# A planner's constant for one transfer's part of the DMA queue: 0.9 in place of 1.1

## The chip, the cores and the metric

The kernel runs on one core of one Trainium2 chip. The metric is the device time of one execution in microseconds, the median of several; three executions of the kernel before took 909.14, 910.29 and 910.53 us. Five engines work beside each other: TensorE (PE in the profile) multiplies matrices into PSUM, VectorE (DVE) and ScalarE (ACT) do elementwise work, and SyncE (SP) and GpSimd (POOL) issue the DMA transfers. Each engine works through its own instructions in the order in which the program was written down, and waits on semaphores for what others have to finish first.

## The reference

Two stages, with 8 sequences of 3,072 tokens, width 256, query and key width 64 and hidden width 1,024:

```python
scores = (1 / S) * z @ z.T                # per sequence, 3072 x 3072
attn   = maximum(scores, 0) ** 2
x      = u * (attn @ v)                   # gated attention, 3072 x 256
h1, h2 = x @ w1, x @ w2                   # 24576 x 1024 each
out    = maximum(h1, h2) @ w_out          # 24576 x 256, float32
```

## The kernel before

A *step* is one block of 512 query tokens of one sequence; there are 48 steps, six to a sequence, numbered through from 0. The scores of a step are made in pairs of 128-token key blocks (`score`, PE), go through a relu and a square (`relu` and `square`, ACT or DVE) and land in SBUF tiles of four key blocks, `a_sb` (a *group*). Since `z @ z.T` is symmetric, a group above the diagonal isn't computed again for the step below it: SyncE transposes it there with a DMA (`turn`, tile `aT`), one transfer for each pair of key blocks. Below, "turn 2:12" is the transfer that turns step 2's key blocks 12 and 13; it goes into group 2 as step 3 reads it, and 2:12 and 2:14 together make up that group. The block on the diagonal has a smaller transfer of its own ("turn 3:diag"). So steps 3, 4 and 5 read what steps 0 to 2 (and the steps just before them) have turned, and nothing is turned for steps 0 to 2.

The products with `v` of steps 0 to 2 are plain matmuls (`plain`). From step 3 on they are made with seven products of quarters in place of eight, in four passes over the groups, `Xa`, `Xb`, `Ya`, `Yb`; the first two read the tiles themselves, the last two also sums of quarters that DVE makes (`es`, jobs `S2` to `S4`), and folded `v` (`lf`). For step 3 the groups are read in the order 0, 1, 4, 5, 2, 3 (the diagonal last), for step 4 in the order 0, 1, 2, 5, 3, 4, for step 5 in the order 5, 0, 1, 2, 3, 4.

The result of a step is multiplied by `u`, which SyncE has turned as well (`uT`), on DVE into `xT` (function `scaled`, `mul_uT`, L295), which also makes the two PSUM accumulators free for the next step's products. A few steps later come the first layer (`d`), a relu (`g`), the second layer (`o`), the copy into `o_sb` (`oc` on ACT, of which there are two buffers, L75) and the store to DRAM, again by SyncE (`store`). `max(h1, h2)` is made as `relu(x (w1 - w2)) @ w_out + x (w2 @ w_out)`; the product `w2 @ w_out` (`w2o`, 16 matmuls in step 3) needs `w2` turned by SyncE (`w2T`, twice the size of a turn).

SyncE's DMAs all go through one queue, in the order in which SyncE issues them (`sp_dma`, L103). The loads of `u`, `v`, `z` and the weights are issued by GpSimd (`load`, L107), most of them tied to a matmul that has to be done first.

No order is written by hand but PE's. Everything else is a *job* with the engines that may do it, a duration, its dependencies and the buffers that it uses. `find_orders` (L1758) is a list scheduler that is run while the program is built: it always takes the job that can begin first, prefers earlier due times among those that can begin within 400 ns, and keeps a clock for each engine and one for the DMA queue (`dma_free`). `settle` (L1773) reckons when a transfer is done: the queue's clock moves on by `DMA_PART` times the transfer's time alone, and SyncE is held back while that clock is over 4,500 ns ahead. `share_wide` (L1835) gives the 19 wide buffers (tiles `a_sb` and `aT`) to their uses by the begins and ends so reckoned; 24 rounds are reckoned, and the order of the best is used (L1879).

```python
dma_free[0] = max(dma_free[0], begin + DMA_START[...]) + DMA_PART * j.dma
j.done = dma_free[0] + DMA_END
if "SP" in j.ways:
    idle_from["SP"] = max(begin + SP_ISSUE, dma_free[0] - DMA_AHEAD)
```

Of the kernel before, what the change touches and what calls it, by code (L numbers as in the profile page):

```python
# [11 lines left out]
def kernel(  # L12
# [185 lines left out]
    TURN, TURN_LAG, UT_LAG = 1750, 4000, 7000  # L198

    DMA = dict(turn=1180, uT=1130, zT=4220, w2T=3800, store=1940, v=1680, u=1680, z=3130, w1=4100, w2=3000, wo=3500)  # L200
    DMA_SMALL, DMA_PART = 970, 1.1
    DMA_START, DMA_END, DMA_AHEAD, SP_ISSUE = {"SP": 870, "POOL": 1770}, 1330, 4500, 1450
    FIRST_LOADS = {("v", 0, 0): 0, ("v", 0, 1): 1200, ("v", 0, 2): 2500, ("v", 0, 3): 3700, ("v", 0, 4): 4900, ("v", 0, 5): 7700, ("u", 0): 6300}

# [1777 lines left out]
```

## Time and profile before

| What | Value |
|---|---|
| Three executions | 909.14, 910.29, 910.53 us |
| Median | 910.29 us |
| Profiled execution, its own time | 914.21 us |
| Profiled execution, span from first to last instruction | 912.4 us |
| PE busy | 892.1 us (98%) |
| DVE busy | 790.0 us (87%) |
| ACT busy | 756.2 us (83%) |
| Mean granted TensorE clock | 0.996 |
| DMAs issued by SyncE | 394, of them 279 turns of score tiles, 48 `uT`, 51 stores |

The span is the time from the first to the last instruction of the profiled execution; its own time of 914.21 us has 1.8 us around that. A row of the timeline gives start, duration, engine, line, operation, what is written and read, how many instructions are merged into the row, and in square brackets the idle time before it and what ended it. SyncE's rows are the issues of transfers; what the profile calls "DMA to landing" is the time from the begin of an issue until the data has landed.

### The profile page before, as it was taken

Reading aid. Unit: us, or ns where it says so; the run is one execution under the profiler, and the core shown is the slowest. Engines: PE = TensorE matmul, PEld = TensorE weight load, DVE = VectorE, ACT = ScalarE, POOL = GpSimd, SP = SyncE. Lnnn points to the kernel's source line nnn. Section 1 sums busy time; section 2 is a strip of 40 time slices with the busy share of each in tenths; the row PEclk is TensorE's granted clock in tenths of the full one; section 3 lists DMA queues with packets and bytes.
Section 4 is the critical chain, followed back from the end, with each engine's and each line's share of the span. In section 5 each row is a group of like instructions: output and inputs, shape, how many; then the busy total and the mean of one; then the engine's idle time right before and its main releaser. Section 6 shows DMA issues by size and latency. Waiting matters only on the chain.

```text
span 912.4 us, 37105 instructions
## 1 busy us (share of the span) xinstructions
PE 892.1 (98%) x16333; PEld 745.5 (82%) x16333; DVE 790.0 (87%) x1703; ACT 756.2 (83%) x944; POOL 58.4 (6%) x115
## 2 busy tenths in 40 slices
PE   9999799999999999999999999999999999999998
PEld 3368688887888888888788888888888898888885
DVE  6777678988989999999899899998999899989970
ACT  7967699778997899888997889977999779997634
POOL 2101000010000000001000010000000001000000
PEclk9999899999999999999999999999999999999999
DMA  9999999999999999999999999999989999999711
GB/s 156 130 167 175 186 182 173 175 163 159 153 169 190 164 183 149 164 185 167 165 146 164 183 169 151 166 169 173 183 138 178 179 178 152 170 160 162 123 61 70
DMA packets 382930, 146.65 MB, mean 161 GB/s; under 512 B 361264, under 2 KB 362928, under 8 KB 382768
## 3 DMA queue, kind: packets, MB, share of 16 engines
q1 hardware_dynamic: 366208, 114.54, 79.3%
q0 software_dynamic: 16560, 29.74, 23.5%
q8 instruction: 127, 2.08, 1.0%
q14 instruction: 35, 0.29, 0.1%
HBM read 59.77 MB, written 25.17 MB: 93 GB/s over the span
## 4 chain that ended last, share of the span: by engine, by line
PE 74%; DVE 12%; DMA 6%; ACT 4%; issue 2%; SPq 0%; POOL 0%; DVEq 0%; POOLq 0%; ACTq 0%
PE s_ps L87 37%; PE acc L87 37%; DMA v_sb<-in_v_dram 3%; DMA aT<-a_sb 3%; DVE es L290 2%; ACT a_sb L276 2%; DVE es L293 2%; DVE a_sb L293 1%; ACT g_sb L276 1%; DVE xT L297 1%; DVE e L290 1%; DVE e L293 1%; DVE a_sb L284 1%; DVE o_sb L293 1%; DVE gs L293 1%
## 5 line engine op out<-in xcount | busy, mean ns | idle before, releaser
L87 PEld LDWEIGHTS <-v_sb 64*128 64x128 bf16 (+1 forms) x4464 | 336.1, 94 | 68.9 <-issue 15.2
L276 ACT ACTIVATE a_sb<-s_ps 128x1024 bf16<-128x1024 f32 x337 | 303.8, 943 | 45.4 <-PE s_ps L87 43.8
L87 PEld LDWEIGHTS <-lf 64*128 64x128 bf16 x3240 | 266.2, 94 | 21.9 <-issue 7.3
L87 PE MATMUL acc<-es,v_sb 64*128 64x256 bf16 x2160 | 279.0, 269 | 0.0
L87 PE MATMUL acc<-es,lf 64*128 64x256 bf16 x1080 | 246.6, 269 | 0.3
L87 PE MATMUL acc<-a_sb,lf 64*128 64x256 bf16 x1224 | 233.1, 269 | 1.0 <-issue 1.0
L87 PE MATMUL s_ps<-xT,w_sb 64*128 64x512 bf16 (+1 forms) x1484 | 214.0, 377 | 0.0
L282 ACT ACTIVATE a_sb<-a_sb 128x1024 bf16<-128x1024 bf16 (+1 forms) x217 | 211.1, 993 | 2.3
L276 ACT ACTIVATE g_sb<-s_ps 128x1024 bf16<-128x1024 f32 x187 | 185.9, 1024 | 8.6 <-PE s_ps L87 6.9
L87 PE MATMUL acc<-aT,lf 64*128 64x256 bf16 x936 | 180.1, 271 | 3.8 <-DMA aT<-a_sb 3.1
L87 PE MATMUL acc<-a_sb,v_sb 64*128 64x256 bf16 (+1 forms) x1352 | 145.4, 280 | 3.2 <-DVE e L290 2.3
L87 PE MATMUL s_ps<-zT 64*128 64x512 bf16 (+2 forms) x774 | 122.5, 337 | 6.1 <-DVE o_sb L290 2.9
L290 DVE TENSOR_TENSOR es<-aT 128x1536 bf16<-128x1536 bf16 (+1 forms) x117 | 106.5, 933 | 1.3 <-DMA aT<-a_sb 1.2
L87 PEld LDWEIGHTS <-gs 64*128 64x128 bf16 x2688 | 99.1, 94 | 9.5 <-issue 1.3
L87 PEld LDWEIGHTS <-w_sb 64*128 64x128 bf16 (+1 forms) x1488 | 80.9, 94 | 26.0 <-POOLq L95 1.0
L87 PEld LDWEIGHTS <-g_sb 64*128 64x128 bf16 x2336 | 91.6, 94 | 10.4 <-POOLq L95 7.1
L284 DVE TENSOR_TENSOR a_sb<-a_sb 128x1024 bf16<-128x1024 bf16 (+1 forms) x121 | 74.8, 625 | 25.9 <-ACT a_sb L276 25.9
L87 PE MATMUL acc<-aT,v_sb 64*128 64x256 bf16 x936 | 89.5, 272 | 0.0
L293 DVE TENSOR_TENSOR es<-a_sb 128x512 bf16<-128x512 bf16 x198 | 79.1, 421 | 9.6 <-PE acc L87 9.5
L87 PE MATMUL s_ps<-wf_sb,gs 64*128 64x128 bf16 x2016 | 81.2, 216 | 0.5 <-issue 0.5
L87 PE MATMUL s_ps<-w_out_sb,g_sb 64*128 64x128 bf16 (+1 forms) x1664 | 78.8, 226 | 0.0
L290 DVE TENSOR_TENSOR es<-a_sb 128x1024 bf16<-128x1024 bf16 x108 | 72.4, 687 | 0.0
(84 smaller groups left out, 1079.6 us busy)
## 6 DMA issues: line engine op xcount, KB each, us to landing
out_dram<-o_sb SPq DMA_DIRECT2D x47, 512.0 KB, 5.5
v_sb<-in_v_dram POOLq DMA_DIRECT2D x48, 256.0 KB, 6.0
u_sb<-in_u_dram POOLq DMA_DIRECT2D x48, 256.0 KB, 5.7
aT<-a_sb SPq DMA_TRANSPOSE x230, 5.3
z_sb<-in_z_dram POOLq DMA_DIRECT2D x7, 384.0 KB, 7.0
w_sb<-in_moe_w_dram POOLq DMA_DIRECT2D x2, 512.0 KB, 10.3
uT<-u_sb SPq DMA_TRANSPOSE x48, 5.6
a_sb<-a_sb SPq DMA_TRANSPOSE x45, 5.5
```

Of the source, the lines that this page charges most:

```text
L87: newest[0] = pin(nc.tensor.matmul(*args, **kw)).ins
L276: pin(nc.scalar.activation(out_ap, in_ap, AF.Relu))
L282: pin(nc.scalar.activation(ap, ap, AF.Square))
L284: pin(nc.vector.tensor_mul(ap, ap, ap))
L290: pin(nc.vector.tensor_add(*args))
L293: pin(nc.vector.tensor_sub(*args))
L297: nc.vector.scalar_tensor_tensor(out=out_ap, in0=in0, scalar=c2, in1=in1, op0=ALU.mult, op1=ALU.mult)
```

## The change

One constant of the planner. With it the planner believes that a transfer takes 0.9 of its time alone in the queue, where it believed 1.1 before: 1,062 ns for a turn in place of 1,298 ns. No instruction is added, removed or made larger.

```diff
-    DMA_SMALL, DMA_PART = 970, 1.1
+    DMA_SMALL, DMA_PART = 970, 0.9
```

The order of PE and of GpSimd stays as it was. The order of SyncE changes in two ways. In the opening, that is up to step 6, it is another order. These are the transfers from the sixth on, before and after, with their places in SyncE's order:

```
place   before     after          place   before     after
  6     1:14       1:14             22    3:16       zT (two)
  7     1:16       1:16             23    3:18       3:16
  8     w2T        1:18             24    0:22       3:18
  9     uT 2       1:20             25    uT 4       0:22
 10     1:18       w2T              26    1:20       2:20
 11     2:12       uT 2             27    1:22       4:diag
 12     2:14       1:22             28    5:diag     2:22
 13     3:diag     0:20             29    2:20       3:20
 14     uT 3       2:12             30    2:22       uT 4
 15     0:16       2:14             31    store 0    5:diag
 16     0:18       0:16             32    3:20       3:22
 17     2:16       3:diag           33    4:20       store 0
 18     2:18       uT 3             34    3:22       4:20
 19     zT (two)   0:18             35    4:22       store 1
 20     0:20       2:16             36    uT 5       4:22
 21     4:diag     2:18             37    6:diag     6:diag
```

From step 7 on the only changes are that of two neighbours in SyncE's order one goes ahead of the other, some five times in each sequence: a `uT` ahead of a turn or of a store, or a turn ahead of a store and a `uT`.

On DVE and ACT the order changes in the opening alone: eight squares of steps 3 to 7 change between the two engines, the first two sums for group 2 of step 3 (`S2`, `S3`) stand ahead of sums for groups 4 and 5, and three folds of `v` of the second sequence stand 28 places earlier. From the middle of step 6 on, both orders are the same as before. The wide buffers are given to 259 of their uses otherwise than before.

## The prediction

> **What bounds the kernel now.** I read the page's busy shares and slices first, then the chain of waits of PE, then the windows around each wait, and last SyncE's rows in the opening.
>
> ```profile
> span 912.4 us, 37105 instructions
> PE 892.1 (98%) x16333; PEld 745.5 (82%) x16333; DVE 790.0 (87%) x1703; ACT 756.2 (83%) x944; POOL 58.4 (6%) x115
> PE   9999799999999999999999999999999999999998
> ```
>
> PE is busy for 892.1 of 912.4 us, and of the 40 slices only the fifth, 91 to 114 us, falls below 9 tenths. So no order of the other engines can save much in the body, but it can lose there, and in the opening (before 114 us) it can do both. These are PE's rows at the waits, and the clock behind them:
>
> ```profile
> 83.09 0.28 PE L87 MATMUL acc<-aT,lf 64*128 64x256 bf16 x2 [0.48 <-DMA aT<-a_sb]
> 103.30 0.39 PE L87 MATMUL s_ps<-zT 64*128 64x512 bf16 x2 [2.18 <-ACT o_sb L287]
> 106.88 0.40 PE L87 MATMUL acc<-aT,lf 64*128 64x256 bf16 x2 [2.65 <-DMA aT<-a_sb]
> 106.00:112.83 6.83, 5.95 (x49) 0.50 1.10 227
> 102.66 1.07 ACT L287 COPY o_sb<-s_ps 128x512 f32<-128x512 f32 x2 [4.39 <-DMA out_dram<-o_sb]
> ```
>
> PE waits 0.48 us for a turn in step 4, 2.18 us for a PSUM pair, and 2.65 us for turn 3:22. The second wait is a transfer's too: ACT's copy, which gives the pair free, waited for store 0 out of `o_sb`. After the two the granted clock is 0.50 from 106.00 to 112.83 us (PE busy 5.95 us there), which costs half of 5.95, 2.97 us. So the opening loses 0.48 + 2.18 + 2.65 + 2.97 = **8.28 us** to late transfers. That is what the change can win, against what it newly makes late.
>
> **The body.** From step 7 on PE, DVE, ACT and GpSimd keep their orders, and SyncE only swaps neighbours. The swapped transfer with the least time to spare, by my reading of all of them, is uT 11:
>
> ```profile
> 213.62 4.24 SPq L104 DMA_TRANSPOSE uT<-u_sb  x1
> DMA to landing us min/median/max: 10.4/10.4/10.4
> 236.93 0.68 DVE L297 SCALAR_TENSOR_TENSOR xT<-e,uT 128x512 bf16<-128x512 f32 x1
> ```
>
> It lands at 224.0 and is read at 236.93, 12.9 us later; a swap moves a transfer by one place, which the issues below put at 1.3 us. If SyncE waits at a `uT` that it reaches too early, the neighbour behind it waits as well, by no more than those 12.9 us allow. At the begins that the trace shows, the new sharing of the wide buffers makes no job after 110 us wait longer. I cost the body at nothing; the cover is this slack, and without it each late transfer would cost PE what it is late by.
>
> **The opening, before.** SyncE issues almost without a pause from 29 to 122 us and is blocked in its issues; the queue sets the pace, so what lands when goes by the place. These are the issues of places 9, 11, 13 to 15, 17, 24, 27, 33 and 36, each with its time to landing (13 is a piece of the chain: begin, length):
>
> ```profile
> L104 SPq DMA_TRANSPOSE uT<-u_sb x1: 1245/1245/1245, 44.5 to 44.5; - x1
> DMA to landing us min/median/max: 8.2/8.2/8.2
> L104 SPq DMA_TRANSPOSE aT<-a_sb x1: 1982/1982/1982, 50.3 to 50.3; - x1
> DMA to landing us min/median/max: 7.9/7.9/7.9
> 57.11 2.77 DMA a_sb<-a_sb
> L104 SPq DMA_TRANSPOSE uT<-u_sb x1: 1263/1263/1263, 58.4 to 58.4; - x1
> DMA to landing us min/median/max: 5.1/5.1/5.1
> L104 SPq DMA_TRANSPOSE aT<-a_held x1: 1294/1294/1294, 59.8 to 59.8; - x1
> DMA to landing us min/median/max: 4.6/4.6/4.6
> L104 SPq DMA_TRANSPOSE aT<-a_sb x1: 1322/1322/1322, 63.7 to 63.7; - x1
> DMA to landing us min/median/max: 3.4/3.4/3.4
> L104 SPq DMA_TRANSPOSE aT<-a_held x1: 1304/1304/1304, 81.1 to 81.1; - x1
> DMA to landing us min/median/max: 3.4/3.4/3.4
> L104 SPq DMA_TRANSPOSE aT<-a_sb x1: 2408/2408/2408, 85.2 to 85.2; - x1
> DMA to landing us min/median/max: 9.6/9.6/9.6
> L104 SPq DMA_TRANSPOSE aT<-a_sb x1: 2130/2130/2130, 100.3 to 100.3; - x1
> DMA to landing us min/median/max: 5.7/5.7/5.7
> L104 SPq DMA_TRANSPOSE uT<-u_sb x1: 1277/1277/1277, 105.8 to 105.8; - x1
> DMA to landing us min/median/max: 3.4/3.4/3.4
> ```
>
> Landings: place 9 at 52.7, 11 at 58.2, 13 at 59.88, 14 at 63.5, 15 at 64.4, 17 at 67.1, 24 at 84.5, 27 at 94.8, 33 at 106.0, 36 at 109.2. An unblocked issue takes 1.24 to 1.32 us, so a turn costs SyncE at least that; the planner's new 1,062 ns is further from it than the old 1,298 ns. It will believe in room that isn't there.
>
> It uses the room for 1:20, 1:22 and 0:20, which steps 4 and later read, at places 9, 12 and 13, ahead of what step 3 waits for. Step 3's rows before:
>
> ```profile
> 52.73 1.29 DVE L297 SCALAR_TENSOR_TENSOR xT<-acc,uT 128x512 bf16<-128x512 f32 x2
> 55.94 0.39 PE L87 MATMUL acc<-aT,v_sb 64*128 64x256 bf16 x4
> 59.22 0.38 PE L87 MATMUL acc<-aT,v_sb 64*128 64x256 bf16 x4
> 60.05 0.36 PE L87 MATMUL acc<-a_sb,lf 64*128 64x256 bf16 x2
> ```
>
> There is no slack: `xT` of step 2 begins at 52.73, as uT 2 lands; group 2 is read at 59.22, turns 2:12 and 2:14 having just landed; the diagonal at 60.05, 0.17 us after 3:diag.
>
> **The change, step by step** (landing = that of the same place before; the bytes ahead of a place are the same to within a turn).
> 1. uT 2 moves from place 9 to 11: 58.2 in place of 52.7. DVE's two `xT` end 1.29 us later, 59.5, and PE's first product of step 3 moves from 55.94 to 59.6: PE idle 3.65 us. Queued behind `xT` on DVE are a square and the sums of step 3, which PE reads later than that.
> 2. Group 2 comes at 59.22 + 3.65 = 62.9 at full clock; 2:12 and 2:14 (places 14 and 15) land at 63.5 and 64.4, up to 1.5 us more.
> 3. 3:diag, place 17, lands at 67.1; with the 0.17 us the row of 60.05 begins at 67.25. Everything so far is inside this: PE is **7.2 us** behind. Below, if the queue paid only the four turns' issues, 4 x 1.3 = 5.2, the wait would be 5.1.
> 4. w2T (place 10) lands before 58.2, and `w2o` comes at 60: nothing; its cover is step 1.
> 5. The clock. Between 55.94 and 67.25 PE idles 3.65 us at once, then some 3.5 in parts, more than the 4.83 us that brought it to 0.50 before. But at 0.50 the work between (about 3.5 us at full clock, 7 at half) just fills the time until 3:diag lands. I take 0 for what the clock costs past 67.25, with 2.97 (the row before) as the upper end.
> 6. The old waits. Turn 3:18 (place 23 to 24, landing 84.5) was wanted at 82.6, now at 89.8: gone, -0.48. Store 0 moves from place 31 to 33, but PE wants its pair at 101.12 - 0.48 + 7.2 = 107.8, and place 33 landed at 106.0: gone, -2.18. 3:22 moves two places ahead: gone, -2.65. With them goes the half clock, -2.97.
> 7. What is late next: 4:22, place 35 to 36. Place 36 landed at 109.2, and since store 1 (twice a turn's bytes) is now ahead of it, about 1.0 later, 110.2. PE wants it at its row of 107.90 (below) less 5.31 of old waits plus 7.2, 109.8: 0.5 us of wait.
> 8. Folds, squares, w2T's and z's later places: their readers move back by 7.2 us too; 0.
>
> ```profile
> 107.90 0.45 PE L87 MATMUL acc<-aT,lf 64*128 64x256 bf16 x2
> 83.42 0.40 PE L87 MATMUL acc<-a_sb,v_sb 64*128 64x256 bf16 x4
> 84.98 0.53 POOL L108 DMA_DIRECT2D v_sb<-in_v_dram  x1 [12.81 <-PE s_ps L87]
> 85.75 0.53 POOL L108 DMA_DIRECT2D u_sb<-in_u_dram  x1 [0.24 <-PE acc L87]
> ```
>
> (The last three rows are for the rival of 4:diag below.) Sum: + 7.2 + 0.5 - 8.28 = **-0.6 us**, against the profiled execution's own 914.21 us (span 912.4). That execution stands 3.9 us above the median, 910.29, so I carry over the difference alone: 909.7 us.
>
> **A rule of the skill on the clock.** The row first: 4.83 us of idle time in two pieces brought 6.83 us of clock 0.50, and the full clock came back only then. The Trainium skill (TensorE: Matmul & The Clock Gate, Part 1: The HAM clock gate) says that the gate looks at free-running windows of about 3.4 us and opens after a busy one. The trace agrees in length (6.83 us is two of them). By that rule the phase of the windows differs from run to run, so that the half clock could outlast 67.25 us or not; the sum would be -0.6 by the one and, as the first rival works out from the rows, +1.9 by the other.
>
> **Rivals.**
> - *The half clock outlasts the wait* (step 5's upper end). For: two idle pieces near 62 and 66 us can close the clock anew after it has opened. Against: at half clock PE has no idle time there. -0.6 + 2.97 less the 0.5 of step 7, which is then covered: +1.9, 912.2 us.
> - *Slower: 4:diag comes late.* It moves from place 21 to 27. PE reads it at 83.42, in the new order at 83.42 - 0.48 + 7.2 = 90.1. Place 27 landed at 94.8; by that PE waits 4.7 us and step 7 nothing: 7.2 + 4.7 - 8.28 = +3.6, 913.9 us. Against: place 27 was late because two loads were issued beside it, at 84.98 and 85.75 us; the rows show that they wait for PE and come 7 us later now. Three issues after place 24's 84.5 it would land at 88.4. It decides if it lands after 90.1.
> - *Faster: the queue is better than its places.* With the wait of 5.1 us from step 3, and 4:22 landing at its old 107.8 (103.9 + 3.9) because the loads are later, step 7 asks for 107.7: 5.2 - 8.28 = -3.1, 907.2 us.
> - *No effect*: the opening's waits trade one for one and the differences of the orders vanish: 910.3 us.
>
> ```profile
> L104 SPq DMA_TRANSPOSE aT<-a_sb x1: 1824/1824/1824, 103.9 to 103.9; - x1
> DMA to landing us min/median/max: 3.9/3.9/3.9
> ```
>
> **How the numbers follow.** Chances: the forecast 0.45, the half clock 0.18, 4:diag 0.17, the better queue 0.13, no effect 0.07. About 0.2% (1.8 us, so 908.5 to 912.1) is what a measurement can tell from no change. The forecast's own range, from step 1 to 3 coming out 1 us shorter or longer, is 908.6 to 911.2, all inside. No effect falls inside too; the half clock lies on the upper bound and is split; 4:diag is slower; the better queue is faster. Faster 0.17, same 0.53, slower 0.30. The range of 8 in 10 reaches from near the better queue to near 4:diag: 907.6 to 913.6 us.
>
> **What would show it.** A gap of 3 to 4 us in PE near 56 us, ended by DVE `xT`, itself waiting for uT; one or two more, ended by DMA `aT` and `a_sb`, before 67 us; a clock of 0.50 near 58 to 68 us and none near 106; no wait at 83, 101 and 104 us; ACT's copy no longer waiting for a store. From 130 us on the rows should stand a constant 0 to 2 us from those before. The prediction is wrong if uT 2 lands by 54 us, if a wait of over 2 us stands between 84 and 100 us, or if the body's waits change by over 1 us.

## The result, and the profile after

The kernel after takes 906.62 us (median of 20 executions). The kernel before, run beside it on the same chip, takes 914.0 us, also the median of 20. The ratio is 0.9932, with a 95% interval of 0.9908 to 0.9956. So the change wins 0.7%, about 6 us. The ratios here and below compare only executions within 1.5% of the fastest of their kernel and the medians count all of them, so that a ratio is not always that of the two medians. The forecast was 909.7 us, 0.07% faster, with "no difference" as the likeliest outcome and a range that ended at 907.6 us (0.3% faster).

The profiled execution of the kernel after took 909.47 us, against 914.21 us of the one before: 4.7 us less, in the span as well (907.7 against 912.4). From the page of the kernel after, the span and the slices of PE:

```profile
span 907.7 us, 37110 instructions
PE   9969999999999999999999999999999999999998
```

The dip of PE has moved from the fifth slice to the third, 45 to 68 us. That is the opening, where the prediction looked. The two rows that follow are the same instruction in both kernels, the first product of step 7 with a turned tile, in PE's timeline (before, then after):

```profile
145.89 0.40 PE L87 MATMUL acc<-aT,v_sb 64*128 64x256 bf16 x4
```

```profile
149.56 0.40 PE L87 MATMUL acc<-aT,v_sb 64*128 64x256 bf16 x4
```

By step 7 the kernel after is 3.67 us *late*. From there to the end of the span it takes 907.7 - 149.56 = 758.1 us, where the kernel before took 912.4 - 145.89 = 766.5 us. So in these two executions the gain of 4.7 us is a loss of 3.7 in the opening and a gain of 8.4 in the body, the part that the prediction costed at nothing.

**The opening.** The waits of PE in the opening of the kernel after, from its timeline:

```profile
59.78 0.37 PE L87 MATMUL acc<-aT,v_sb 64*128 64x256 bf16 x1 [5.47 <-DVE xT L297]
60.37 0.58 PE L87 MATMUL acc<-aT,v_sb 64*128 64x256 bf16 x3 [0.23 <-DVE xT L297]
66.72 0.39 PE L87 MATMUL acc<-aT,v_sb 64*128 64x256 bf16 x4 [1.19 <-DMA aT<-a_sb]
68.13 0.29 PE L87 MATMUL acc<-aT,lf 64*128 64x256 bf16 x2 [1.01 <-DMA aT<-a_sb]
70.44 0.38 PE L87 MATMUL acc<-a_sb,v_sb 64*128 64x256 bf16 x3 [1.94 <-DMA a_sb<-a_sb]
70.56 0.36 PE L87 MATMUL acc<-a_sb,lf 64*128 64x256 bf16 x2
```

The first five are the predicted waits in the predicted order: `xT` of step 2, the turns of group 2, the diagonal. The last row is the one that began at 60.05 before. Behind them stands the queue. The next rows are the issues of uT 2 and of 3:diag in the kernel after, each with its time to landing, and then DVE's `xT` from the timeline:

```profile
L104 SPq DMA_TRANSPOSE uT<-u_sb x1: 1933/1933/1933, 42.7 to 42.7; - x1
DMA to landing us min/median/max: 16.2/16.2/16.2
L104 SPq DMA_TRANSPOSE a_sb<-a_sb x1: 1243/1243/1243, 67.5 to 67.5; - x1
DMA to landing us min/median/max: 2.9/2.9/2.9
```

```profile
59.03 1.29 DVE L297 SCALAR_TENSOR_TENSOR xT<-acc,uT 128x512 bf16<-128x512 f32 x2 [9.65 <-DMA uT<-u_sb]
```

uT 2 lands at 42.7 + 16.2 = 58.9 us and 3:diag at 67.5 + 2.9 = 70.4. The granted clock of the kernel after, from the windows (begin and end, length and PE's busy time in it, clock, DMA share, GB/s):

```profile
57.21:64.04 6.83, 4.03 (x20) 0.50 1.38 68
64.04:70.87 6.83, 2.69 (x37) 1.00 0.98 192
70.87:74.28 3.41, 3.41 (x36) 0.50 1.16 144
```

The clock falls to 0.50 twice. In the first stretch PE is working from 59.78 on, but what it gets done later by that is covered: at 66.72 it still waits 1.19 us for a turn. The second begins after the last wait and finds PE busy throughout (3.41 of 3.41 us), so it costs half of that, 1.7 us. The waits of before at 83.09, 103.30 and 106.88 us are gone, and so is the half clock that stood behind them.

**The body.** PE's waits from 150 to 900 us (who waits for whom: us in total, times, longest), first of the kernel before, then of the kernel after:

```profile
PE s_ps L87 <- DVE o_sb L290: 2.9, 5, 0.6
PE acc L87 <- issue: 2.5, 4, 1.0
PE acc L87 <- DVE e L290: 2.3, 3, 1.7
PE s_ps L87 <- issue: 1.0, 2, 0.5
```

```profile
PE s_ps L87 <- DVE o_sb L290: 0.6, 1, 0.6
PE acc L87 <- DVE e L290: 0.4, 1, 0.4
```

8.7 us of waits have become 1.0 us. Two kinds have gone: waits for DVE (5.2 to 1.0 us) and waits that the profile puts down to nothing ("issue", 3.5 to none). The first kind comes at one place of a sequence, and in the kernel before in sequences 3 to 7 (they are numbered from 0). This is sequence 4 in the kernel before: the issue of its last load of `v`, who waited for it and its time to landing, then rows of the timelines of SyncE, DVE and PE:

```profile
L108 POOL DMA_DIRECT2D v_sb<-in_v_dram x1: 528/528/528, 445.1 to 445.1; - x1
  DVE lf L290: 2.4, 1
DMA to landing us min/median/max: 7.9/7.9/7.9
```

```profile
445.69 0.33 SPq L104 DMA_DIRECT2D out_dram<-o_sb  x1
446.69 3.56 SPq L104 DMA_TRANSPOSE uT<-u_sb  x1
453.19 0.42 DVE L290 TENSOR_TENSOR lf<-v_sb 128x512 bf16<-128x512 bf16 x1 [2.40 <-DMA v_sb<-in_v_dram]
455.72 0.40 PE L87 MATMUL acc<-a_sb,v_sb 64*128 64x256 bf16 x4 [1.72 <-DVE e L290]
```

And the same place in the kernel after, the load and SyncE's rows:

```profile
L108 POOL DMA_DIRECT2D v_sb<-in_v_dram x1: 531/531/531, 446.3 to 446.3; - x1
DMA to landing us min/median/max: 5.2/5.2/5.2
```

```profile
447.88 1.23 SPq L104 DMA_TRANSPOSE uT<-u_sb  x1
449.22 1.09 SPq L104 DMA_DIRECT2D out_dram<-o_sb  x1
```

Before, SyncE issues a store 0.6 us behind the load, and the load takes 7.9 us to land. DVE's fold of `v` waits 2.40 us for it. DVE is late for `e`, and PE waits 1.72 us for that. After, `uT` goes ahead of the store, the store is issued 2.9 us behind the load, the load takes 5.2 us, and nobody waits for it. Over sequences 2 to 7 this load takes 5.1, 6.5, 7.9, 6.2, 6.6 and 5.8 us before (mean 6.4), and 6.6, 4.8, 5.2, 5.1, 4.9 and 5.1 after (mean 5.3). In sequence 2 of the kernel after, the one that stays long, a wait remains (1.06 us of DVE's fold); the one 0.6 and the one 0.4 us of PE above are of that sequence.

The difference in the load isn't that of two executions. In the four profiles in which SyncE issues the store 0.6 us behind the load (before, e2, e4 and e8 below) the load takes 6.5 us on average (24 loads, 4.9 to 8.4). In the five in which the store comes 2.9 to 4.9 us behind it (after, e1, e3, e6, e7) it takes 5.3 us (30 loads, 4.7 to 6.6).

### The profile page after: what moved, and what is told of

It is laid out like the page before. It is cut to its first block, busy times and chain, and to the rows that moved or that the text cites. A ratio compares the mean times of both kernels' runs of the same rounds, so it can differ in the third digit from the quotient of the medians.

```text
span 907.7 us, 37110 instructions
## 1 busy us (share of the span) xinstructions
PE 890.0 (98%) x16333; PEld 744.3 (82%) x16333; DVE 788.7 (87%) x1701; ACT 754.1 (83%) x946; POOL 58.6 (6%) x115
## 4 chain that ended last, share of the span: by engine, by line
PE 76%; DVE 11%; ACT 7%; DMA 3%; issue 2%; SPq 1%; DVEq 0%
PE acc L87 38%; PE s_ps L87 38%; ACT a_sb L276 2%; ACT g_sb L276 2%; DVE es L290 2%; DMA uT<-u_sb 2%; DVE es L293 2%; DVE a_sb L293 1%; DVE xT L297 1%; ACT a_sb L282 1%; DVE e L290 1%; DVE o_sb L293 1%; DVE e L293 1%; SPq L104 1%; DMA v_sb<-in_v_dram 1%
## 5 line engine op out<-in xcount | busy, mean ns | idle before, releaser
L87 PE MATMUL s_ps<-zT 64*128 64x512 bf16 (+2 forms) x774 | 120.5, 334 | 2.0 <-DVE o_sb L290 0.6
```

Of the source, the lines that this page charges most:

```text
L87: newest[0] = pin(nc.tensor.matmul(*args, **kw)).ins
```

## The experiments

The theory after the result: six of the swaps, a `uT` ahead of the store four steps back, take that store away from beside the last load of `v`; the rest of the gain, if any, comes from the other swaps, and the opening gives little or nothing. The first rival: the opening won it, and the body's difference is chance. The second: it isn't that store, but some other swap, or all of them a little.

All experiments change only the finished order, with one helper that moves a job behind another one (two `assert` lines of it are left out here). In all of them the whole computation is made.

```diff
+    def behind(first, second):
+        keys = [j.key for j, _ in emitted]
+        i, k = keys.index(first), keys.index(second)
+        held_back = emitted.pop(i)
+        emitted.insert(k, held_back)
```

The runs of one group share a chip and the executions of the kernel before (911.23 us for e1 to e4, 910.41 for e5 to e8, 911.16 for e9 and e10):

```
run                    median us   ratio to before [95%]
e1 all body swaps        903.6     0.9946 [0.9914, 0.9977]
e2 opening only          912.23    1.0018 [0.9988, 1.0049]
e3 six stores            907.29    0.9967 [0.9937, 0.9997]
e4 other 26 swaps        909.08    0.9975 [0.9937, 1.0012]
e5 early load            904.58    0.9941 [0.9911, 0.9972]
e6 later loads           905.93    0.9963 [0.9937, 0.9988]
e7 turns back            908.33    0.995  [0.991,  0.999]
e8 stores back           910.02    1.0003 [0.9971, 1.0034]
e9 turns and early load  903.25    0.9924 [0.9892, 0.9956]
e10 swaps and early load 900.97    0.9907 [0.9876, 0.9937]
```

**e1: the body's change alone.** The kernel before with all 32 swaps of the body; its opening is untouched.

```diff
+    swaps = [(("turn", 7, 22), ("uT", 8)), (("turn", 47, None), ("uT", 46))]
+    for n in range(NG, len(steps), NG):
+        if n + NG < len(steps):
+            swaps += [(("store", n - 1), ("turn", n + 2, 22)), (("turn", n + 3, 22), ("uT", n + 4))]
+            swaps += [(("turn", n + 6, 4), ("uT", n + 5)), (("store", n + 2), ("uT", n + 6)), (("turn", n + 7, 22), ("uT", n + 8))]
+    for first, second in swaps:
+        behind(first, second)
```

> The kernel before, its opening and buffers unchanged, with all 32 swaps of neighbours in SyncE's order from step 7 on. If the gain comes from the body (the two profiles: the changed kernel is 3.5 us behind at 116 us and 4.9 us ahead at 793 us, 8.5 us won between), 5 to 9 us less than the kernel before, and less than the changed kernel as well. If the body's waits are chance and the gain is the opening's, or none, as the prediction has it: within 1 us of the kernel before.

Ratio 0.9946, faster. PE's waits from 150 to 900 us are those of the kernel after to a tenth:

```profile
PE s_ps L87 <- DVE o_sb L290: 0.6, 1, 0.6
PE acc L87 <- DVE e L290: 0.3, 1, 0.3
```

The neighbours' swaps alone win 4.9 us of the 6 that the change wins, at the lower end of the 5 to 9 expected.

**e2: the opening's change alone.** The kernel after with the same 32 swaps undone.

```diff
+    for first, second in swaps:
+        behind(second, first)
```

> The changed kernel with the 32 swaps of the body undone, so that only the opening (and the sharing of the wide buffers) differs from the kernel before. If the gain is the body's: 2 to 5 us more than the kernel before, from the later opening. If it is the opening's: 5 us less.

Ratio 1.0018, no difference that can be told. PE's waits from 150 to 900 us are back:

```profile
PE acc L87 <- DVE e L290: 4.5, 4, 2.2
PE s_ps L87 <- DVE o_sb L290: 3.4, 6, 0.6
PE s_ps L87 <- issue: 0.9, 1, 0.9
PE acc L87 <- issue: 0.6, 1, 0.6
```

With e1 this rules out the first rival. The opening, which was all of the forecast, is worth +0.18% [-0.12, +0.49], +1.6 us. The two parts, -4.9 and +1.6, make -3.3 us in place of the -6 of the whole change, which the intervals allow.

**e3: six stores.** The kernel before; only the six stores go behind the `uT` that follows them.

```diff
+    for b in range(2, B):
+        behind(("store", NG * b - 4), ("uT", NG * b))
```

> The kernel before with six of the 32 swaps alone: stores 8, 14, 20, 26, 32 and 38, each behind the uT that follows it. In the profile of before these six are issued 0.5 us after the last load of v of a sequence, which then takes 5.1 to 7.9 us, and the fold of v on DVE waits for it up to 2.4 us; in the changed kernel it takes 4.8 to 5.2 us in five of six sequences. If the store beside that load is the cause: 4 to 7 us less than before, nearly as much as all 32 swaps. If not: within 1 us of before.

Ratio 0.9967, faster, but by 3.0 us in place of the 4 to 7 expected. PE's waits from 150 to 900 us:

```profile
PE acc L87 <- issue: 1.8, 3, 0.8
PE s_ps L87 <- DVE o_sb L290: 1.0, 3, 0.4
PE s_ps L87 <- issue: 0.6, 2, 0.5
```

Six swaps of 32 take the waits for DVE from 5.2 to 1.0 us, as far as the whole change does, and the load of sequence 4 lands after 4.8 us. The "issue" waits stay.

**e4: the other 26.** The kernel before with the swaps of e1, without these six.

```diff
+    for first, second in swaps:
+        if (first[0], second[0]) != ("store", "uT"):
+            behind(first, second)
```

> The kernel before with the other 26 swaps alone (turns and uT, and a store behind a turn). If the six stores are the cause: within 1.5 us of before. If the gain lies in the body, but not in the six stores: 4 to 8 us less.

Ratio 0.9975, 2.3 us less with an interval that reaches from 5.7 less to 1.1 more: not decided between the two. The waits for DVE are there as before, 3.1 and 2.1 us, and no "issue" wait is:

```profile
PE s_ps L87 <- DVE o_sb L290: 3.1, 5, 0.6
PE acc L87 <- DVE e L290: 2.1, 3, 1.4
```

**e8: the stores back.** The kernel after; only the six stores go ahead of their `uT` again.

```diff
+    for b in range(2, B):
+        behind(("uT", NG * b), ("store", NG * b - 4))
```

> The changed kernel with the six stores ahead of their uT again, as before. If the six stores make the gain of the body: the fold waits again for the load of v in most sequences, 3 to 5 us more than the changed kernel, so 1 to 4 us less than before. If they don't: as the changed kernel, 6 us less than before.

Ratio 1.0003: without the six swaps the change wins nothing that can be measured. The load and the waits are those of before (the load of sequence 4, who waited for it, and PE's waits from 150 to 900 us):

```profile
L108 POOL DMA_DIRECT2D v_sb<-in_v_dram x1: 528/528/528, 437.6 to 437.6; - x1
  DVE lf L290: 1.9, 1
DMA to landing us min/median/max: 7.5/7.5/7.5
```

```profile
PE acc L87 <- DVE e L290: 2.9, 3, 1.2
PE s_ps L87 <- DVE o_sb L290: 2.9, 5, 0.6
PE s_ps L87 <- issue: 1.7, 1, 1.7
PE acc L87 <- issue: 0.3, 1, 0.3
```

So the six swaps are sufficient for the waits for DVE to go (e3) and without them the waits come back (e8). The second rival falls as far as the waits for DVE go.

**e5: the load in place of the store.** If the store harms by delaying the load, the stores can stay where they are and the load can go earlier. The kernel before; the last load of `v` of sequences 2 to 7 is issued right behind the one before it.

```diff
+    for b in range(2, B):
+        keys = [j.key for j, _ in emitted]
+        load_v = emitted.pop(keys.index(("v", b, 0)))
+        emitted.insert(keys.index(("v", b, NG - 1)) + 1, load_v)
```

> The kernel before, SyncE's order untouched; GpSimd issues the last load of v of sequences 2 to 7 right behind the one before it, some 4 to 5 us earlier, so that it is not alone with the store. If the late landing of this load, beside the store, is what DVE's fold and then PE wait for: the fold's waits (up to 2.4 us) and PE's waits after it go, 3 to 5 us less than before, as with the six stores. If the store matters for another reason (SyncE held up, buffers): within 1.5 us of before.

Ratio 0.9941. No swap is made, and PE waits for DVE nowhere from 150 to 900 us:

```profile
PE s_ps L87 <- issue: 3.5, 5, 2.0
PE acc L87 <- issue: 0.4, 2, 0.2
```

That shows the chain: what counts for these waits is when the load lands, not the store as such. The load now takes 7.1 to 9.4 us, beside other loads and the store, but it is issued some 5 us earlier and lands before DVE wants it: no fold of sequences 2 to 7 waits for its load.

**e6: later loads in the opening.** e1, and three loads of steps 4 and 5, which lie beside store 0 and turn 3:22, are issued later, as is the fold that reads the first of them.

```diff
+    behind(("fold", 1, 1, 0), ("S4", 5, 4))
+    behind(("v", 1, 4), ("score", 6, 14))
+    behind(("u", 5), ("o", 2, 0))
+    behind(("v", 1, 5), ("Xb", 5, steps[5].groups[0]))
```

> The kernel before with all 32 swaps of the body, and in step 4 and 5 three loads of GpSimd later: v 1:4 (behind a score of step 5 at 103 us in place of 85), u 5 (behind o of step 2, 96 in place of 86), v 1:5 (109 in place of 90), and the fold that reads the first behind a sum of step 5. If the opening's waits at 103 and 107 us come from the queue's load by then: 2 to 4 us less than with the swaps alone, so 7 to 9 us less than before. If the loads cost the turns nothing: the same as with the swaps alone; if they land too late for step 6, more.

Ratio 0.9963, 3.4 us less than before in place of the 7 to 9 expected, and not better than e1. From 75 to 150 us PE no longer waits for a turn or for `o_sb`, but 2.0 us for `g_sb` and 1.5 us for other things. In this profile the old waits have gone with what ran beside the queue, and new ones of the same size (3.5 us, where e1 has 3.4) have come in their place. One execution doesn't show more than that.

**e7: three turns back.** The kernel after; 1:20, 1:22 and 0:20 go behind 3:diag, so that 2:12, 2:14 and 3:diag move three places up, and uT 2, which only 1:20 of them stood ahead of, one.

```diff
+    for key in (0, 20), (1, 22), (1, 20):
+        behind(("turn", *key), ("turn", 3, None))
```

> The changed kernel with turns 1:20, 1:22 and 0:20 behind 3:diag, where step 3 no longer waits for them. By the prediction's steps 1 to 3 the wait in step 3 falls from 10 us (profile of the changed kernel) to 1 to 5, and that of step 5 comes back in part: 0 to 5 us less than the changed kernel, 6 to 11 us less than before. If the opening's total is set by the queue alone: the same as the changed kernel, 6 us less than before.

The waits of step 3 are gone (none from 50 to 75 us, where the kernel after has 9.8 us), and others come back later (75 to 150 us):

```profile
PE acc L87 <- DMA a_sb<-a_sb: 2.5, 1, 2.5
PE acc L87 <- DMA aT<-a_sb: 0.5, 1, 0.5
```

With the three turns ahead PE waits 4.2 to 9.8 us in step 3 (the kernel after, e2, e8), and with them back not at all (e7, e9). So these turns are what makes step 3 wait in the new order, as steps 2 and 3 of the prediction say. That uT 2 is what is waited for, as step 1 says, isn't so in each execution: with the same order it lands at 58.9 us in the kernel after, at 54.4 in e2 (PE waits 1.5 us for `xT`), and in e8 at 38.5 + 5.4 = 43.9 us, where nobody waits for it. From e8, the issue of uT 2 and its time to landing:

```profile
L104 SPq DMA_TRANSPOSE uT<-u_sb x1: 1626/1626/1626, 38.5 to 38.5; - x1
DMA to landing us min/median/max: 5.4/5.4/5.4
```

The time is 4.6 us less than before in place of the 6 to 11 expected. Whether that is better than the kernel after isn't decided: 0.995 [0.991, 0.999] against 0.9932, from different groups of runs.

**e9 and e10: a faster version.** e9 is e7 with the early load of e5, e10 is e1 with it; the edits are the same.

> The changed kernel with two edits: the three turns 1:20, 1:22 and 0:20 go behind 3:diag again, and the last load of v of sequences 2 to 7 is issued right behind the one before it. If the body's loss is the late fold and the opening's loss is the late uT 2, and the two are separate, both go: no wait of over 1 us in step 3, no wait of DVE's folds in sequences 2 to 7, PE idle in the body under 1.5 us beside the issue waits, and 902 to 905 us against 910 to 911 of the kernel before (ratio 0.990 to 0.995). If the six stores' places had done all that could be done in the body (rival), the early load adds nothing and it stays at the 0.995 of the run with the turns alone.

> The kernel before with all 32 swaps of the body and the early load, its opening untouched. If the swaps and the early load take away the same wait (DVE's late fold), their gains don't add up: 903 to 906 us, ratio 0.992 to 0.996, as each alone (0.9946 and 0.9941). If they are two gains, it comes out near 0.989, 900 to 901 us.

e9 gives 0.9924, with no wait of PE in step 3 and none of DVE's folds in sequences 2 to 7, as expected if the two losses are separate. e10 gives 0.9907 [0.9876, 0.9937], 900.97 us, the lowest median of all. In its profile PE waits for nothing from 150 to 900 us. Both beat the kernel before; over the kernel after (0.9932 [0.9908, 0.9956]) the intervals overlap, so that e10 beats it too isn't shown. Whether the swaps and the early load add up isn't either: 0.9907 lies between what each gives alone and the product of both, 0.9887.

**The opening varies from execution to execution.** PE's waits in step 3 (50 to 75 us) and later in the opening (75 to 150 us), from the waits view of each profile, ordered by SyncE's order in the opening:

```
order of before    before 0 / 5.3   e1 3.8 / 3.4   e3 2.6 / 4.4   e4 4.4 / 1.1   e5 1.5 / 1.6   e10 2.7 / 4.8
order of after     after 9.8 / 0    e2 8.0 / 0     e8 4.2 / 0
three turns back   e7 0 / 3.0       e9 0 / 4.9
```

(e6, whose loads in the opening are moved, is left out.) The new order does what the prediction said: it trades the late waits (1.1 to 5.3 us, none with the new order) for longer waits in step 3. But the profile of before, on whose rows the prediction rests, is the only one of the old order without a wait in step 3. So one execution's rows aren't the opening's price: the sums are 3.1 to 7.5 us for the old order (mean 5.9) and 4.2 to 9.8 for the new one (mean 7.3). The difference, 1.4 us, is near the 1.6 us of e2, but with three profiles of the new order it is no more than a hint.

Each execution's result also has its mean granted clock. One stretch of 3.41 us at 0.50 lowers the mean over 908 us by 0.0019, so that 0.998 is about one stretch and 0.996 two. The executions of before beside the experiments took 907.6 us on average at 1.000 (9 executions), 909.6 at 0.998 (29), 912.3 at 0.996 (30), 913.6 at 0.994 (3). A fit over the 190 of these executions that the ratios count (a mean for each kernel and each group of runs, and a price for each stretch) gives 2.4 us a stretch, with a 95% interval of 0.4 to either side. It also gives each kernel's difference from before at the same number of stretches:

```
e1 all body swaps   -6.0 +- 1.6      e5 early load            -5.7 +- 1.7
e3 six stores       -3.4 +- 1.6      e7 turns back            -6.2 +- 1.9
e4 other 26 swaps   -1.8 +- 1.7      e8 stores back           -0.8 +- 1.7
e2 opening only     +0.3 +- 1.7      e9 turns and early load  -7.0 +- 1.7
e6 later loads      -3.8 +- 1.6      e10 swaps and early load -9.1 +- 1.9
```

The stretches are on average 1.4 in the kernel before; with the new opening they are 2.0 in the kernel after and in e2, and 1.6 in e8. At 2.4 us a stretch, 0.2 to 0.6 more of them make 0.5 to 1.4 us, and e2 has nothing beside that can be told. The fit is a correlation: the waits that bring a stretch are part of the 2.4 us, so that it doesn't show that the clock is what the new opening costs.

## Why the prediction was wrong

**The step that failed** is the part on the body: "I cost the body at nothing; the cover is this slack". For each swapped transfer it asked whether the transfer itself would land in time for its reader, and that held: PE waits for no transfer in the body of the kernel after. It didn't ask what a moved transfer runs *beside*. A store that goes behind a `uT` is not read by anyone, but it uses the DMA engines at the time when a load of GpSimd's is under way, and that load had no slack: DVE's fold waited for it. In place of 0 the body gave -0.54% [-0.86, -0.23] (e1), -4.9 us, or -6.0 +- 1.6 us at the same number of half-clock stretches. By the latter measure the six stores give -3.4 +- 1.6 us, with the chain shown at each link (load, fold, `e` and `o_sb`, PE). The other 26 swaps give -1.8 +- 1.7 us, with no chain shown. The prediction had named a sign for this failure, "if the body's waits change by over 1 us": they went from 8.7 to 1.0 us. That the forecast, -0.6 us, points the way that the time went is luck: it was added up in the opening, and the opening alone measured +1.6 us.

The profile of before had the hint. 8.7 us of PE's waits lie behind 150 us, more than the 5.3 us that the prediction found in the opening, and DVE waits there for `v_sb` (4.3 us in all, 3 times, by the waits view of before). The prediction read the page's slices, in which all of the body stands at 9, and took that for an engine without waits: it said "no order of the other engines can save much in the body". A slice of 23 us shows 9 with a wait of 2 us in it.

The Trainium skill (DMA: Bandwidth & Descriptors, Issuing engines are not separate DMA queues) says that DMAs of all issuing engines run on the same 16 engines and interleave. The trace agrees: the same load takes 7.9 us with SyncE's store 0.6 us behind it, and 5.2 with it 2.9 us behind. By that rule a swap of two transfers of SyncE's concerns each transfer of GpSimd's that is under way.

**Step 1** (uT 2): the place was right, and the time came out in the profiled execution. Predicted to land at 58.2, landed at 58.9; PE's first product of step 3 predicted at 59.6, began at 59.78. The wait is 5.47 in place of 3.65 us only because PE was there 1.6 us earlier in this execution; the product came 3.84 us later than in the profile of before. The agreement is in part luck: with the same order uT 2 lands at 54.4 us in e2 and at 43.9 in e8.

**Steps 2 and 3** (group 2 and the diagonal): the waits came, 1.19, 1.01 and 1.94 us, but the size was off. 3:diag landed at 70.4 in place of 67.1, and PE is 70.56 - 60.05 = 10.5 us behind in place of 7.2. The price of a place in the queue was taken from one execution. (The row of 60.05 isn't quite the first that reads the diagonal: PE's first product with it begins inside the row before, at 59.92 us, 0.04 us after 3:diag has landed. That changes the sum by 0.1 us.)

**Step 4** (`w2T`): nothing waited for it, as said.

**Step 5** (the clock): "I take 0 for what the clock costs past 67.25" was wrong in this execution. The first rival happened in half: a second stretch after the wait, 1.7 us in place of 0 or 2.97.

**Step 6** (the old waits): right, -8.28 us, and in all three profiles with the new order none of them is left. But e3, e4 and e5 show that before's 5.3 us in those waits and none in step 3 is one outcome of several of the old order.

**Step 7 and the other rivals**: 4:22 was not waited for (0 in place of 0.5, for which step 7's own numbers give 0.4), nor was 4:diag. The better queue did not come; in the profiled execution the queue was worse.

The steps as measured in the two profiles sum to +10.5 + 1.7 - 8.3 = +3.9, and the row of step 7 shows +3.67. So in the opening the mechanism and the order of the waits were right for the profiled execution, and the sum of -0.6 was 4.3 us too low for that execution, 2.2 us too low against e2, inside the interval of e2.

**Open.** The "issue" waits of PE in the body are 1.5 to 3.9 us in the four profiles without the 26 other swaps (before, e2, e3, e5) and none in four with them (after, e1, e4, e10), but 0.4 to 2.9 us in the other four that have them as well (e6 to e9). Whether these swaps take them away isn't settled, nor what PE waits for in them.

## What to carry to other kernels

Before an order is called harmless in a stage, list the stage's waits, however full its slices look, and follow each back to the transfer at its root; here waits of under 2 us, a few in each sequence, added up to 8.7 us, more than the waits of the opening. For a transfer that is moved, ask not only who reads it, but which transfers of other engines are under way at its old and its new place, and how much time their readers have. And look at the spread of executions before a sum to tenths is made from one: here a stretch of half clock more or less is 2.4 us, four times the forecast.

## What the runs showed of the hardware

A load of 256 KB from GpSimd that takes 4.8 to 5.2 us in most sequences of the kernel after takes 5.1 to 7.9 us, 6.4 on average, in the kernel before, where a store of 512 KB from SyncE is issued 0.6 us behind it. In the opening a transfer can take far longer, and the time varies from execution to execution: uT 2 took 16.2 us to land in the kernel after and 5.4 in e8 with the same order of SyncE up to it, where the median of its kind is 4.9 in the kernel after, by its page's rows of DMA issues (count, us to landing):

```profile
uT<-u_sb SPq DMA_TRANSPOSE x48, 4.9
```

The clock fell to 0.50 at 70.87 us after 6.83 us in which PE was busy for 2.69 us but never idle for more than 1.94 us at once. The Trainium skill (TensorE: Matmul & The Clock Gate, Why this matters for your kernels) advises against idle gaps over about 3 us; here shorter ones did it when they added up to 4.14 us (6.83 - 2.69), and the measurement decides. That the stretches are 3.41 and 6.83 us long agrees with the windows of about 3.4 us of that page's Part 1.
